# Aligning TensorE's tiles to 128 bytes and reading the output weights from the last column to the first

## The chip, the cores and the metric

One core of one Trainium2 chip runs the whole program. The metric is the device time of one execution in microseconds (us); before the change the median of three runs is 708.79 us (708.63 to 709.17).

## The reference

An attention block with 32 memory slots feeds a two-layer network. Per batch b (8), head h (8), with 576 tokens s, 64 channels d and 32 slots m:

```
a    = exp(phi - max_s phi);  a = a / (sum_s a + 1e-9)
k_m  = a^T k;   v_m = a^T v                       # 32 x 64 per head
attn = softmax over m of (q k_m^T / 8)            # 576 x 32 per head
x    = attn v_m, heads side by side               # 4608 tokens x 512
h    = x @ w_in                                   # 512 x 2048
g    = h if h > 0 else exp(h) - 1
out  = g @ w_out                                  # 2048 x 512
```

## The kernel before, in words

Batches run one after another; each one's 576 tokens are two halves of 288. The attention of a batch gives `A`, its probabilities (128 rows of head and slot, two groups). `x` is never formed: `vw` is v_m times w_in, four tiles per batch of 512 of the 2048 hidden channels each (`vw(b, c)`, L722 to L742), and the hidden layer is `vw` times `A`.

The main loop goes over 256 steps: (batch, half, j), where j is one of 16 blocks of 128 hidden channels. `hidden` (L769) makes a 128 x 288 block in PSUM from six matmuls: three passes over two groups, with high and low parts (`PASSES`, L40) of 4-byte float32r operands; the stationary operand is a 128 x 128 piece of `vw`, the moving one 288 columns of `A`. ScalarE (L793, L794) and VectorE (L802, L805) apply the activation into a `gf` tile (five buffers), and L825 and L831 split it into the high and low parts of a `gp` tile. `project` (L847) then calls `by_channels` (L837) for two blocks of 128 tokens: three matmuls each, where the stationary operand is a 128 x 128 piece of `gp` and the moving one 512 columns of `wout[j]`, its high or low part. The last 32 tokens of each half are gathered over two batches in a `rest` tile, and go through `by_channels` in `rest_project` (L892). So L839 runs 256 x 6 + 4 x 16 x 3 = 1728 times, and L778 256 x 6 = 1536 times.

TensorE loads the stationary operand by an instruction of its own (PEld in the profile) ahead of each matmul. The order of all work is written out by hand: the table `FIRST` for the first batches and `at(place, ...)` for the others.

The weights come as 64-bit words, `w_in` and `w_out`, and are decoded on the chip while the first two batches run (L390 to L441). `dec_high` and `dec_rest` leave `wout[j]` as [128, 2, 512]: high and low part, 512 output columns each. All tiles lie in SBUF for the whole program. Pools lay them one behind another in units of 32 bytes, so a small tile (`tiny`, `nm`, `rinv`, `mx`, `rs`, the `touch` targets) shifts all that follow. The four `touch` DMAs at the start (L922) load 64 bytes per partition that nothing reads, each into a tile of its own.

Of the kernel before, what the change touches and what calls it, by code (L numbers as in the profile page):

```python
# [8 lines left out]
F32 = mybir.dt.float32  # L9
# [7 lines left out]
P = 128  # L17
B, H, S, D, M = 8, 8, 576, 64, 32
DM, DFF = 512, 2048
HALF = S // 2  # L20
# [10 lines left out]
NJ = DFF // P  # L31
# [142 lines left out]
def fused_kernel(ctx: ExitStack, tc: tile.TileContext, phiT, phi, phit, kv0, kvt, kv, q0, q1, w_in, w_out, out):  # L174
# [11 lines left out]
    work = ctx.enter_context(tc.tile_pool(name="work", bufs=2))  # L186
# [9 lines left out]
    wout = {}  # L196
# [262 lines left out]
    def slot_scale(b):  # L459
        s = st[b]  # L460
        sums = s["sums"]
        nc.vector.tensor_scalar(sums, sums, EPS, None, ALU.add)
        rinv = work.tile([P, 2], F32, name="rinv")
        nc.vector.reciprocal(rinv, sums)
        s["rinv"] = rinv

# [180 lines left out]
    def softmax_sum(b, u):  # L647
        sc = st[b]["sc"][u]
        n = sc.shape[1]
        sm = work.tile([P, 2 * HALF // SQ], F32, name="sm")[:, :n]  # L650
        nc.vector.tensor_reduce(sm, sc, AX.X, ALU.add)
        nc.vector.tensor_scalar(sm, sm, EPS, None, ALU.add)
        rs = work.tile([P, 2 * HALF // SQ], F32, name="rs")[:, :n]
        nc.vector.reciprocal(rs, sm)
        st[b]["rs", u] = rs

# [180 lines left out]
    def by_channels(ps, gp, j, first, last):  # L837
        for n, (x, y) in enumerate(PASSES):
            nc.tensor.matmul(  # L839
                ps,  # L840
                gp[:, y],
                wout[j][:, x, :],
                start=(first and n == 0),
                stop=(last and n == 2),
            )

    def project(it):  # L847
        b, hf, j = order[it]
        _, first, last = ends[it]
        if first:  # L850
            acc[b, hf] = [ps_o.tile([P, DM], F32, name=f"pso{hf}{t}") for t in range(NT)]
        gp = gps.pop(it)
        for t in range(NT):
            by_channels(acc[b, hf][t], gp[:, :, t * P : (t + 1) * P], j, first, last)
# [37 lines left out]
    def rest_project(p, i):  # L892
        if i == 0:
            acc["rest", p] = ps_o.tile([P, DM], F32, name="pso00")
        gp = gs.pop(("rest", p, i))[1]
        for n in range(2):
            j = 2 * i + n
            by_channels(acc["rest", p], gp[:, :, n * P : (n + 1) * P], j, j == 0, j == NJ - 1)

    def rest_store(p):  # L900
# [4 lines left out]
        for n in range(4):  # L905
            eng[n % 2].dma_start(
                out[2 * p + n // 2, n % 2, NT * P :], t[n * REST : (n + 1) * REST, :]
            )

    tiny = work.tile([P, 1], F32, name="tiny", bufs=1)  # L910
    warm = ps_o.tile([P, P], F32, name="pso00")

    touched = {
# [5 lines left out]
        "out": w_out[0][:, :8],  # L919
    }  # L920

    def touch(x):  # L922
        rows = touched[x]
        n = 16 * list(touched).index(x)
        t = work.tile([P, 16], F32, name=f"touch{n}", bufs=1)
        if x in ("in", "out"):
            t, rows = t.bitcast(U32), rows.bitcast(U32)
        nc.scalar.dma_start(t, rows)
# [4 lines left out]
    def warm_up(n):  # L933
# [7 lines left out]
        f.__name__: f  # L941
        for f in (
            tables, touch, warm_up, load_phi, load_e, load_kv, load_kv0, load_q, load_half_q, load_raw, dec_mag,
            dec_sign, dec_low, dec_top, dec_add, dec_high, dec_rest, phi_max, phi_exp, slot_scale,
            spread_max, e_shift, e_exp, e_transpose, e_copy, slots, slots_copy, slots_transpose,
            kv_copy, clear, scores, scores_of, turn, softmax_max, softmax_shift, softmax_exp, softmax_sum,
            softmax_divide, back, turn_back, probs_high, probs_low, vw, vw_high, vw_low, hidden,
            elu_exp, elu_max, elu_rest, rest_copy, elu_high, elu_low, project, collect, store, rest_high, rest_low,
# [18 lines left out]
    def softmax(b, u, o, *steps):  # L967
        turned, shifted, exped, divided, back, parts = (o + x for x in steps)
        at(turned, turn, b, u)
        at(shifted, softmax_max, b, u)  # L970
        at(shifted + 0.01, softmax_shift, b, u)
        at(exped, softmax_exp, b, u)
        at(divided, softmax_sum, b, u)
        at(divided + 0.01, softmax_divide, b, u)
        at(back, turn_back, b, u)
        at(parts, probs_high, b, u)
        at(parts + 0.01, probs_low, b, u)
# [8 lines left out]
    def attention(b, o):  # L986
        at(o + 0.5, load_phi, b)
        for u in range(3):
            at(o + 1 + 0.1 * u, load_e, b, u)
        at(o + 3.5, phi_max, b)  # L990
        at(o + 3.6, spread_max, b)
        for c in range(NCH):
            at(o + 3.7 + 0.01 * c, load_kv, b, c)
        at(o + 3.8, load_q, b, 0)
        for g in range(2):
            at(o + 5.5 + g, phi_exp, b, g)
        at(o + 7.5, slot_scale, b)
        for u in range(3):
            at(o + 8, e_shift, b, u)
            at(o + 9.5 + u, e_exp, b, u)  # L1000
        for c in range(NCH):
            at(o + 12.4, slots, b, c)
        at(o + 12.5, load_q, b, 1)
        at(o + 12.6, load_q, b, 2)
        at(o + 13.5, slots_copy, b)
        at(o + 14.4, slots_transpose, b)
        at(o + 14.5, kv_copy, b)
        at(o + 17.4, scores_of, b, "bb", "wx")
        for u in range(3):
            softmax(b, u, o + 18.5 + 2.5 * u, 0, 1, 2, 3, 4, 5)  # L1010
# [86 lines left out]
```

## Time and profile before

| | |
|---|---|
| runs, median (lowest to highest) | 708.79 us (708.63 to 709.17) |
| span of the profiled execution, first to last instruction | 706.7 us |
| TensorE matmul (PE) busy | 697.6 us, 99% |
| TensorE weight load (PEld) busy | 581.0 us, 82% |
| VectorE (DVE) busy | 453.0 us, 64% |
| ScalarE (ACT) busy | 457.0 us, 65% |
| GpSimd (POOL) busy | 69.4 us, 10% |

The profile gives a span and no separate time for its own execution; what lies around the span (start and completion) is taken as the 2.1 us between 706.7 and the median of 708.79. The busy time of PE includes the modelled end of each matmul, which runs on while the next one streams, so the pace of matmuls is read from the starts of consecutive rows and not from their lengths.

### The profile page before, as it was taken

To read this page: it belongs to the slowest core of one execution; us is meant where nothing else is said; L and a number is where in the kernel's file an instruction comes from. 1 tells how busy PE (TensorE), PEld (TensorE's weight loads), DVE (VectorE), ACT (ScalarE), POOL (GpSimd) and SP (SyncE) were. 2 spreads that over 40 slices of the span, in tenths; PEclk is the share of its full clock that TensorE was granted. 3 is DMA by queue.
4 is the path that set the end of the run, shared out by engine and by line. 5 is a ranking of instruction groups with operands and counts; after the bars stand their busy time and mean duration, and the time that the engine had idled before them with its cause. 6 is when DMAs were issued, how large, how long until landed. Compare 5 with 4: busy or idle time off the path is not lost.

```text
span 706.7 us, 13637 instructions
## 1 busy us (share of the span) xinstructions
PE 697.6 (99%) x5112; PEld 581.0 (82%) x5112; DVE 453.0 (64%) x1207; ACT 457.0 (65%) x1101; POOL 69.4 (10%) x117
## 2 busy tenths in 40 slices
PE   8999999999999999999999999999999999999997
PEld 7778787878878888888787888878888888788886
DVE  4989877976686469554864548764683546944442
ACT  3879988877457557575655746765564655756652
POOL 0332342123000200020000200001000010000000
PEclk9999999999999999999999999999999999999999
DMA  9982023351314400251003420243001440000001
GB/s 344 406 349 90 1 68 116 113 154 23 134 43 109 171 31 2 97 177 64 1 1 111 165 76 1 66 105 137 31 1 59 106 157 31 1 31 0 31 2 45
DMA packets 26450, 64.50 MB, mean 91 GB/s; under 512 B 3984, under 2 KB 8592, under 8 KB 26384
## 3 DMA queue, kind: packets, MB, share of 16 engines
q1 hardware_dynamic: 25712, 63.46, 26.3%
q8 instruction: 41, 0.67, 0.4%
q10 hardware_dynamic: 672, 0.16, 0.1%
q14 instruction: 25, 0.20, 0.1%
HBM read 54.17 MB, written 9.44 MB: 90 GB/s over the span
## 4 chain that ended last, share of the span: by engine, by line
PE 94%; DMA 4%; DVE 0%; ACT 0%; issue 0%; SPq 0%
PE pso L839 57%; PE psh L778 29%; PE psb L556 4%; PE psb L497 2%; PE pso L556 2%; DMA raw<-w_out 2%; DMA raw<-w_in 1%; DMA qh<-q 1%; DMA touch<-kv 0%; PE psb L525 0%; PE psb L569 0%; PE pso L569 0%; PE psh L672 0%; SPq L322 0%; DVE A L715 0%
## 5 line engine op out<-in xcount | busy, mean ns | idle before, releaser
L839 PE MATMUL pso<-wout,gp 128*128 128x512 f32 x1728 | 440.0, 395 | 0.0
L839 PEld LDWEIGHTS pso<-wout,gp 128*128 128x128 f32 x1728 | 310.9, 188 | 61.3 <-issue 2.1
L778 PEld LDWEIGHTS psh<-A,vw 128*128 128x128 f32 x1536 | 227.6, 188 | 33.8 <-issue 9.2
L778 PE MATMUL psh<-A,vw 128*128 128x288 f32 x1536 | 245.9, 297 | 0.6 <-ACT A L701 0.4
L793 ACT ACTIVATE gf<-psh 128x288 f32<-128x288 f32 x256 | 105.2, 411 | 104.6 <-PE psh L778 99.2
L805 DVE SCALAR_TENSOR_TENSOR gf<-gf,psh 128x256 f32<-128x256 f32 x192 | 80.7, 421 | 140.0 <-ACT gf L794 139.8
L825 ACT CAST gp<-gf 128x256 fp32r<-128x256 f32 x256 | 103.4, 405 | 76.9 <-DVE gf L805 65.2
L831 DVE TENSOR_TENSOR gp<-gf,gp 128x256 fp32r<-128x256 f32 x256 | 112.4, 442 | 51.1 <-ACT gp L825 50.1
L794 ACT ACTIVATE gf<-gf 128x288 f32<-128x288 f32 x256 | 114.2, 446 | 8.1
L298 POOL TENSOR_TENSOR e<-e,nmb 128x512 f32<-128x512 f32 x12 | 16.5, 1397 | 361.5 <-ACT gf L794 160.5
L802 DVE SCALAR_TENSOR_TENSOR gf<-gf,psh 128x288 f32<-128x288 f32 x64 | 28.6, 450 | 17.7 <-ACT gf L794 15.9
L813 DVE SCALAR_TENSOR_TENSOR rest<-gf,psh 128x32 f32<-128x32 f32 x192 | 34.6, 180 | 0.0
L740 DVE TENSOR_TENSOR vw<-psb,vw 128x512 fp32r<-128x512 f32 (+2 forms) x48 | 27.0, 584 | 4.4 <-ACT vw L734 4.4
L883 ACT CAST gp<-rest 128x256 fp32r<-128x256 f32 x32 | 12.6, 406 | 21.9 <-PE pso L839 21.9
L821 POOL COPY rest<-gf 128x32 f32<-128x32 f32 x64 | 18.8, 320 | 70.2 <-DVE gf L802 70.1
L734 ACT CAST vw<-psb 128x512 fp32r<-128x512 f32 (+2 forms) x48 | 22.5, 498 | 0.7 <-PE psb L556 0.7
L888 DVE TENSOR_TENSOR gp<-rest,gp 128x256 fp32r<-128x256 f32 x32 | 12.9, 420 | 15.6 <-ACT gp L883 15.6
L556 PE MATMUL psb<-win,kvm 64*32 64x512 f32 (+2 forms) x384 | 22.3, 521 | 0.0
L396 ACT ACTIVATE mag<-raw 128x512 uint32<-128x512 uint32 x30 | 20.1, 672 | 2.6 <-DVE win L418 1.3
L392 ACT ACTIVATE mag<-raw 128x512 f32<-128x512 f32 x30 | 19.7, 669 | 0.6 <-DMA raw<-w_in 0.4
L740 DVE TENSOR_TENSOR vw<-pso,vw 128x512 fp32r<-128x512 f32 (+1 forms) x28 | 17.2, 625 | 0.7 <-ACT vw L734 0.6
L734 ACT CAST vw<-pso 128x512 fp32r<-128x512 f32 (+1 forms) x28 | 14.5, 530 | 0.5 <-PE pso L556 0.5
(134 smaller groups left out, 443.5 us busy)
## 6 DMA issues: line engine op xcount, KB each, us to landing
kvt<-kv SPq DMA_DIRECT2D x32, 512.0 KB, 7.6
raw<-w_in SPq DMA_DIRECT2D x15, 512.0 KB, 9.6
raw<-w_out SPq DMA_DIRECT2D x15, 512.0 KB, 9.0
out<-osb SPq DMA_DIRECT2D x14, 512.0 KB, 2.8
qt<-q SPq DMA_DIRECT2D x18, 384.0 KB, 4.4
ph<-phiT SPq DMA_DIRECT2D x7, 576.0 KB, 4.9
e<-phi SPq DMA_DIRECT2D x12, 256.0 KB, 4.6
kvt<-kvt SPq DMA_DIRECT2D x8, 256.0 KB, 8.1
```

The source lines that it names most:

```text
L556: nc.tensor.matmul(outs[a][32 * j : 32 * j + 32, :], lhs[r, 32 * j : 32 * j + 32], rhs[r, j], start=True, stop=True, tile_position=(64 * a ...
L734: nc.scalar.copy(s["vw"][c][:, HI, a, n0:n1], s["ps"]["vw", c, n0][a])
L740: nc.vector.tensor_tensor(t[:, LO, a, n0:n1], s["ps"]["vw", c, n0][a], t[:, HI, a, n0:n1], ALU.subtract)
L778: nc.tensor.matmul(ps, t[:, x, g, c0 : c0 + P], s["A"][hf][:, y, g, :], start=(n == 0), stop=(n == 5),)
L793: nc.scalar.activation(gf, ps, AF.Relu, scale=-1.0)
L794: nc.scalar.activation(gf, gf, AF.Exp, scale=-1.0)
L802: nc.vector.scalar_tensor_tensor(gf, gf, -1.0, ps, ALU.add, ALU.max)
L805: nc.vector.scalar_tensor_tensor(gf[:, :n], gf[:, :n], -1.0, ps[:, :n], ALU.add, ALU.max)
L813: nc.vector.scalar_tensor_tensor(rest_of(b, j)[:, o : o + REST], gf[:, n:], -1.0, ps[:, n:], ALU.add, ALU.max)
L825: nc.scalar.copy(gp[:, HI], gs[it][:, : NT * P])
L831: eng.tensor_tensor(gp[:, LO], gf[:, : NT * P], gp[:, HI], ALU.subtract)
L839: nc.tensor.matmul(ps, gp[:, y], wout[j][:, x, :], start=(first and n == 0), stop=(last and n == 2),)
```

## The change

Small pads bring every tile that TensorE reads to a multiple of 128 bytes. The `touch` DMAs write into the first `gf` tile in place of four tiles of their own. `w_out` is handed to the kernel with its columns reversed, and the matmul of L839 reads the 512 columns of `wout[j]` with a step of -1, from the last to the first, so that its results come out in the same order as before. The instructions of each engine stand in the same order as before, with the same operations and shapes.

```
@@ slot_scale
         rinv = work.tile([P, 2], F32, name="rinv")
+        pad("rinv", 64)
@@ softmax_sum
         rs = work.tile([P, 2 * HALF // SQ], F32, name="rs")[:, :n]
+        pad("rs", 64)
@@ by_channels
                 ps,
                 gp[:, y],
-                wout[j][:, x, :],
+                wout[j][:, x, ::-1],
@@ before the steps
+    pads = set()
+    def pad(name, n):
+        if name not in pads:
+            pads.add(name)
+            work.tile([P, n // 4], F32, name=f"pad_{name}", bufs=1)
     tiny = work.tile([P, 1], F32, name="tiny", bufs=1)
+    pad("tiny", 96)
@@ touch
-        t = work.tile([P, 16], F32, name=f"touch{n}", bufs=1)
+        if not spots:
+            spots.append(work.tile([P, HALF], F32, name="gf", bufs=5))
+        t = spots[0][:, n : n + 16]
@@ kernel
-        "w_out": np.ascontiguousarray(moe_w_out).view(np.uint64).reshape(NJ, P, DM),
+        "w_out": np.ascontiguousarray(moe_w_out[:, ::-1]).view(np.uint64).reshape(NJ, P, DM),
```

Where the tiles start, as the remainder of the byte address after division by 128, in the programs as built:

| tile | read by | before | changed |
|---|---|---|---|
| `A` (4 buffers) | L778, moving | 32 | 0 |
| `vw`, pool of three buffers | L778, stationary | 0 | 0 |
| `vw` of c = 3 from batch 2 on | L778, stationary | 32 | 0 |
| `gp` (3 buffers) | L839, stationary | 32 | 0 |
| `wout` 0 to 7 and 12 to 15 | L839, moving | 32 | 0 |
| `wout` 8 to 11 | L839, moving | 96 | 0 |
| `ident`, `win` | transposes, products | 0 | 0 |
| `kvm`, e tiles | products, slots | 96 | 0 |
| `ph`, key, value and query tiles | transposes, slots, scores | 32 | 0 |

## Rows read from the trace of the kernel before

**Rows 1.** The page: busy time by engine, granted clock, chain by engine and line.
```profile
span 706.7 us, 13637 instructions
...
PE 697.6 (99%) x5112; PEld 581.0 (82%) x5112; DVE 453.0 (64%) x1207; ACT 457.0 (65%) x1101; POOL 69.4 (10%) x117
...
PEclk9999999999999999999999999999999999999999
...
PE 94%; DMA 4%; DVE 0%; ACT 0%; issue 0%; SPq 0%
PE pso L839 57%; PE psh L778 29%; PE psb L556 4%; PE psb L497 2%; PE pso L556 2%; DMA raw<-w_out 2%; DMA raw<-w_in 1%; DMA qh<-q 1%; DMA touch<-kv 0%; PE psb L525 0%; PE psb L569 0%; PE pso L569 0%; PE psh L672 0%; SPq L322 0%; DVE A L715 0%
```

**Rows 2.** Groups of the page: line, engine, operation, count; busy us, mean ns; idle before.
```profile
L839 PE MATMUL pso<-wout,gp 128*128 128x512 f32 x1728 | 440.0, 395 | 0.0
L839 PEld LDWEIGHTS pso<-wout,gp 128*128 128x128 f32 x1728 | 310.9, 188 | 61.3 <-issue 2.1
L778 PEld LDWEIGHTS psh<-A,vw 128*128 128x128 f32 x1536 | 227.6, 188 | 33.8 <-issue 9.2
L778 PE MATMUL psh<-A,vw 128*128 128x288 f32 x1536 | 245.9, 297 | 0.6 <-ACT A L701 0.4
```

**Rows 3.** Timeline of PE: start us, us, line, count; `vw` at remainder 0.
```profile
299.14 0.96 PE L778 MATMUL psh<-A,vw 128*128 128x288 f32 x6
299.94 1.56 PE L839 MATMUL pso<-wout,gp 128*128 128x512 f32 x6
301.34 0.96 PE L778 MATMUL psh<-A,vw 128*128 128x288 f32 x6
302.14 1.55 PE L839 MATMUL pso<-wout,gp 128*128 128x512 f32 x6
303.53 0.96 PE L778 MATMUL psh<-A,vw 128*128 128x288 f32 x6
```

**Rows 4.** The same view further on, where L778 reads `vw` of c = 3.
```profile
310.09 0.94 PE L778 MATMUL psh<-A,vw 128*128 128x288 f32 x6
310.87 1.54 PE L839 MATMUL pso<-wout,gp 128*128 128x512 f32 x6
312.25 0.94 PE L778 MATMUL psh<-A,vw 128*128 128x288 f32 x6
313.03 1.54 PE L839 MATMUL pso<-wout,gp 128*128 128x512 f32 x6
314.40 0.94 PE L778 MATMUL psh<-A,vw 128*128 128x288 f32 x6
```

**Rows 5.** Timeline of PE: warm-up matmuls of `ident` with `ident`, both at remainder 0.
```profile
25.12 2.50 PE L935 MATMUL pso<-ident 128*128 128x128 f32 x20
27.37 1.04 PE L778 MATMUL psh<-A,vw 128*128 128x288 f32 x6
```

**Rows 6.** Pieces of the chain: start us, us, what; two long runs of L839.
```profile
530.69 12.59 PE pso L839 x54
543.28 0.80 PE psh L778 x6
...
687.68 15.13 PE pso L839 x66
```

**Rows 7.** Busy us (instructions) by stretch: the decoding of the weights, and later.
```profile
20.00:60.00 40.00, 37.95 (x405) 31.52 (x398) 35.16 (x89) 33.54 (x83) 13.12 (x18) 1.00 0.78 310
60.00:150.00 90.00, 89.93 (x558) 74.38 (x558) 78.77 (x162) 79.47 (x186) 27.53 (x48) 1.00 0.30 95
350.00:450.00 100.00, 100.00 (x685) 83.40 (x684) 61.59 (x178) 61.81 (x153) 3.66 (x4) 1.00 0.19 63
```

**Rows 8.** L839 alone by stretch: PE busy, PEld busy, clock, DMA share, GB/s.
```profile
20.00:60.00 40.00, 11.09 (x42) 7.45 (x42) 1.00 0.78 310
60.00:100.00 40.00, 25.52 (x102) 18.49 (x102) 1.00 0.17 54
100.00:150.00 50.00, 31.68 (x126) 22.80 (x126) 1.00 0.41 128
```

More of the change, by code (lines that the diff above doesn't have):

```diff
@@ L920, in fused_kernel @@
     }
+    spots = []
     def touch(x):
```

## The prediction

> **What bounds the kernel now.** I read the page first. TensorE's matmuls are busy for 99% of the span, and the chain that ended last is TensorE for 94% of it: L839, the output product, alone 57% and L778, the hidden layer, 29% [rows 1]. [...] The groups then show that these matmuls wait for nobody: idle time before L839 is 0.0 us over 1728 instructions, before L778 0.6 us over 1536 [rows 2]. What is left is the pace inside TensorE, from one matmul's start to the next, and this is the only thing that the change can move much.
>
> The timeline gives that pace. Six matmuls of L839 start at 302.14 and the next group starts at 303.53: 1.39 us, or 231.7 ns each [rows 3]. Six of L778 take 301.34 to 302.14, or 133.3 ns each. [...] The long runs in the chain say the same: 12.59 us for 54 is 233.1 ns, 15.13 us for 66 is 229.2 ns [rows 6]. [...] The weight load is 188 ns against a pace of 231.7 for L839, with 61 us of idle time over the program before it [rows 2], so it fits beside the stream of L839. [...]
>
> **The change, part by part.** No instruction is added, removed or moved on any engine's queue, and every shape stays. The `touch` DMAs keep their number and size. They now hold the first `gf` buffer: the buffer is taken again only when the other four have been used, steps after 64 bytes per partition have landed, so I cost this and the pads at nothing. If that cover failed, it would be one wait, once. The reversed `w_out` arrives as the same contiguous words, decoding works column by column, and the reversal on the way in is undone by the reversed read; nothing for the other engines.
>
> *Alignment, L778.* Before, `A` starts at remainder 32 and three of four `vw` tiles at 0; from batch 2 on the fourth tile is at 32, like `A`. The trace therefore holds the experiment already: with different remainders six matmuls take 0.80 us (299.14 to 299.94, and 301.34 to 302.14) [rows 3], with equal ones 0.78 us (310.09 to 310.87, and 312.25 to 313.03) [rows 4]. The changed kernel has equal remainders everywhere. 48 of the 256 groups (six batches, two halves, four j) have them already, so 208 x 0.02 = 4.2 us. Whether remainder 0 is better than 32 for both is not shown; bounds for this term are 0 and 4.2 doubled, and I take 4.
>
> *Alignment, L839.* `gp` and 12 of the 16 `wout` tiles have equal remainders already. The groups beside the two kinds of `vw` take 1.40, 1.39 and 1.38, 1.37 us [rows 3, 4], too little to carry a term. Nothing.
>
> *Reversal, L839.* No row shows a descending read. [...] Between nothing and 21.8 I take 8 ns x 1728 = 13.8 us: the pace of 229.2 to 233.1 in rows with different buffers shows that some of the excess depends on where operands lie, but the `ident` row has half the fetch rate and may flatter the floor.
>
> The gain is not all kept. 270 of the 1728 matmuls of L839 run between 20 and 150 us [rows 8], where VectorE and ScalarE are busy for 87 to 88% of 60 to 150 us while they decode weights [rows 7]. There a faster TensorE soon waits for them, and I take back nearly all that these 270 would give, 270 x 8 ns = 2.2, say 2 us. Later both are at 62%, and a TensorE that is 2 to 3% faster leaves them at 64%.
>
> Sum: 706.7 - 4 - 13.8 + 2 = 690.9 us of span; with the 2.1 us around it 693.0. The median of the runs is 708.8, which is the same 2.1 above the span, so the forecast compares directly.
>
> [...] The pace differs by 3 ns per matmul of L778 with the stationary tile's place [rows 3, 4], so the two reads of TensorE seem not to be free of each other. [...]
>
> **The rivals.**
> *Only the alignment works.* Direction is immaterial, L778 gains its 4.2 us, L839 stays at 231.7: 704.6. For it: this is the only part with rows behind it. [...]
>
> [...]
>
> *The descending stream is slower.* The place is the fetch of `wout` in L839, all 1728 times. It decides as soon as a backward read costs more than 4.2 us / 1728 = 2.4 ns per matmul. [...] For it: nothing else in the program reads backwards, so nothing shows that the fetch can. Against it: L839 already leaves its weight load room, and a step of -1 touches the same bytes.
>
> **How the numbers follow.** Forecast (both parts, the reversal worth between 3 and 22 us): 0.52. Alignment alone: 0.18. Nothing: 0.13. Slower: 0.17. A measurement of this kernel can tell about 0.2% from no change, 1.4 us; so faster is 0.52 + 0.18 = 0.70, same 0.13, slower 0.17. Within the forecast the reversal gives, if the floor of the `ident` row is reached and alignment pays double, 693.0 - (21.8 - 13.8) - 4 = 681.0, and 677 if L778 then loses another 4 / 1536 us of its 13 ns each, 2.6 ns; I start the range there. Upwards it takes in alignment alone (704.6) and no change (708.8 and its scatter): 711. Left out are nearly all of the slower rival and a little below, under 2 in 10.
>
> **What would show it.** In the timeline six matmuls of L839 should take 1.34 us or so where they took 1.39 or 1.40, and six of L778 0.78 everywhere; the busy time of the L839 group should fall from 440 to about 426. L839 still at 1.39 with L778 at 0.78 means alignment alone. [...] New idle time before L839 or L778 between 20 and 150 us would show the taken-back part. The prediction is wrong if L839's pace moves the other way, or if the excess of L778 falls far below 10 ns, since I give it 10.

## The result and the profile after

The changed kernel is slower: 713.78 us (713.45 to 714.10, four runs) against 708.87, a ratio of 1.0071 with a 95% interval of 1.0059 to 1.0083. The forecast was 693, the range 677 to 711.

The page after, with the same parts as [rows 1] and [rows 2] (the lines of the kernel have moved: L839 is L841, L778 is L780):

```profile
span 711.7 us, 13639 instructions
...
PE 702.9 (99%) x5112; PEld 581.8 (82%) x5112; DVE 455.1 (64%) x1207; ACT 456.6 (64%) x1101; POOL 69.3 (10%) x117
...
PE 94%; DMA 4%; DVE 0%; ACT 0%; issue 0%; SPq 0%
...
L841 PE MATMUL pso<-wout,gp 128*128 128x512 f32 x1728 | 445.4, 399 | 0.0
L841 PEld LDWEIGHTS pso<-wout,gp 128*128 128x128 f32 x1728 | 310.5, 188 | 64.8 <-issue 2.1
...
L780 PE MATMUL psh<-A,vw 128*128 128x288 f32 x1536 | 246.3, 298 | 0.6 <-ACT A L703 0.4
```

The span grew by 5.0 us. The busy time of the output product grew by 5.4, from 440.0 to 445.4, that of the hidden layer by 0.4, and no idle time came up in front of either. So nearly all of the loss is inside one group of 1728 matmuls. Its pace, the mean distance from a start to the next over all matmuls whose successor starts within 300 ns, went from 231.0 to 233.9 ns: 2.9 x 1728 = 5.0 us. The hidden layer's (within 200 ns) went from 132.9 to 133.3.

The timeline of PE after, in the same place as [rows 3]:

```profile
300.57 0.96 PE L780 MATMUL psh<-A,vw 128*128 128x288 f32 x6
301.37 1.56 PE L841 MATMUL pso<-wout,gp 128*128 128x512 f32 x6
302.77 0.96 PE L780 MATMUL psh<-A,vw 128*128 128x288 f32 x6
303.57 1.56 PE L841 MATMUL pso<-wout,gp 128*128 128x512 f32 x6
304.97 0.96 PE L780 MATMUL psh<-A,vw 128*128 128x288 f32 x6
```

The two groups of L841 take 1.40 us each, 233.3 ns a matmul. Such a pair of rows hides how regular this has become: before, the middle half of the distances lay between 228 and 233 ns, after it lies between 233 and 234. The long runs show the loss best; the chain after has, for the two pieces of [rows 6],

```profile
533.90 12.81 PE pso L841 x54
...
692.33 15.46 PE pso L841 x66
```

12.81 against 12.59 us and 15.46 against 15.13, 4 and 5 ns for each matmul. The prediction named this as a sign of being wrong: L839's pace moved the other way.

### The profile page after: what moved, and what is told of

Its sections match the earlier page's. It is cut to its first block, busy times and chain, and to the rows that moved or that the text cites. A ratio compares the mean times of both kernels' runs of the same rounds, so it can differ in the third digit from the quotient of the medians.

```text
span 711.7 us, 13639 instructions
## 1 busy us (share of the span) xinstructions
PE 702.9 (99%) x5112; PEld 581.8 (82%) x5112; DVE 455.1 (64%) x1207; ACT 456.6 (64%) x1101; POOL 69.3 (10%) x117
## 4 chain that ended last, share of the span: by engine, by line
PE 94%; DMA 4%; DVE 0%; ACT 0%; issue 0%; SPq 0%
PE pso L841 57%; PE psh L780 29%; PE psb L557 4%; PE psb L498 2%; PE pso L557 2%; DMA raw<-w_out 2%; DMA raw<-w_in 1%; DMA qh<-q 1%; DMA gf<-kv 0%; PE psb L526 0%; PE psb L570 0%; PE pso L570 0%; PE psh L674 0%; SPq L322 0%; DVE A L717 0%
## 5 line engine op out<-in xcount | busy, mean ns | idle before, releaser
L841 PE MATMUL pso<-wout,gp 128*128 128x512 f32 x1728 | 445.4, 399 | 0.0
L841 PEld LDWEIGHTS pso<-wout,gp 128*128 128x128 f32 x1728 | 310.5, 188 | 64.8 <-issue 2.1
L780 PEld LDWEIGHTS psh<-A,vw 128*128 128x128 f32 x1536 | 228.4, 188 | 34.9 <-issue 9.2
L780 PE MATMUL psh<-A,vw 128*128 128x288 f32 x1536 | 246.3, 298 | 0.6 <-ACT A L703 0.4
L425 POOL TENSOR_TENSOR top<-top,mag 128x512 uint32<-128x512 uint32 x9 | 12.5, 1391 | 24.8 <-ACT mag L396 24.8
```

Of the source, the lines that this page charges most:

```text
L780: nc.tensor.matmul(ps, t[:, x, g, c0 : c0 + P], s["A"][hf][:, y, g, :], start=(n == 0), stop=(n == 5),)
L841: nc.tensor.matmul(ps, gp[:, y], wout[j][:, x, ::-1], start=(first and n == 0), stop=(last and n == 2),)
```

## The experiments

**One half of the change at a time.** Two kernels split it: the first has the pads and the `touch` targets without the reversal, the second the reversal without the pads.

```
e1: the changed kernel with
-                wout[j][:, x, ::-1],
+                wout[j][:, x, :],
-        "w_out": np.ascontiguousarray(moe_w_out[:, ::-1])...
+        "w_out": np.ascontiguousarray(moe_w_out)...
e2: the kernel before with these two lines the other way
```

> Only the alignment: pads and the touch targets as in the change, w_out stored and read forward. Theory R (the backward read is what costs): L839's line keeps about 231 ns from start to start and the time is 708.8 or, with the 4 us of the hidden layer, 705. Theory A (the places cost: both operands of a matmul now start at the same multiple of 128): L839's line goes to 233 to 234 ns as in the changed kernel and the time is 713 to 714. Theory B (only the two together cost): as R.

> Only the reversal, tiles where they were before. Theory R: 233 to 234 ns per matmul of L839's line and 713 to 714 us, the same for wout 8 to 11 (remainder 96) and the others (32). Theory A: 231 ns and 708 to 709 us. Theory B (weights are read back to front too, so two descending streams that start at the same remainder stay in step and collide all along): wout 8 to 11 leave the 233 ns, by several ns, and the others keep it.

The alignment alone gives 708.20 us, ratio 0.9995 (0.9985 to 1.0004): nothing that can be told from no change. The reversal alone gives 714.06 us, ratio 1.0075 (1.0060 to 1.0090): all of the loss. The same two rows of the chain, of e1 and then of e2:

```profile
530.09 12.61 PE pso L841 x54
...
687.13 15.09 PE pso L841 x66
```

```profile
534.36 12.78 PE pso L839 x54
...
692.79 15.43 PE pso L839 x66
```

The pace of the output product is 230.6 ns in e1 and 234.0 in e2. Theory R stands, theory A falls for these places. In e2 `wout` 8 to 11, at another remainder than `gp`, keep 233.5 ns like the others at 234.2, which already speaks against theory B.

**Is it a collision of two backward streams?** Theory B supposes that the weight load runs back to front as well, which no row shows either way: then both reads of the changed kernel ran backward, and tiles at the same remainder might stay in step and collide. Two kernels move `gp` by 64 bytes, one with the backward `wout`, one with the forward one.

```
e5: the changed kernel, e6: e1, both with
     def elu_high(it):
+        pad("gp_ahead", 64)
         gp = work.tile([P, 2, NT * P], F32R, name="gp", bufs=3)
+        pad("gp_behind", 64)
```

> The changed kernel with gp, the stationary operand of the output product, 64 bytes further on (remainder 64 against wout's 0), still read against reversed wout. Theory R: still 233 to 234 ns and 713 to 714 us, whatever the offset. Theory B: the streams no longer collide, the pace falls below 228 ns and the time below 705 us.

> As e1 (aligned, read forward), with gp at remainder 64 against wout's 0. Theory R: as e1, since two streams that run against each other meet at any offset: 230 to 232 ns. Theory A: the pace falls from 233 to 231 ns or less as the remainders part.

e5: 712.67 us, ratio 1.0058 (1.0041 to 1.0075), pace 233.4 ns. The backward read keeps its pace with the streams out of step, far from the 228 ns and 705 us of theory B, which falls as the cause of the loss. A small part of it may stand: the changed kernel, with both tiles at remainder 0, reads `wout` 8 to 11 at 234.9 ns and the others at 233.6, e5 at 233.1 and 233.4, and is 1.1 us faster. e6: 707.99 us, ratio 0.9984 (0.9975 to 0.9994), pace 231.4 ns, with the hidden layer at 132.0 in place of e1's 133.3.

**The disputed cost by itself (e7, the probe).** At the end of the kernel before, eleven runs of 40 matmuls, each with an own line, on the high part of `wout[5]`; forward and backward by turns. Both directions read the same tile with the same contents, so nothing but the direction differs within a pair.

```
+        w = wout[5][:, HI, :]
+        run(lambda o, g: nc.tensor.matmul(o, g, w, start=True, stop=True))
+        run(lambda o, g: nc.tensor.matmul(o, g, w[:, ::-1], start=True, stop=True))
...
```

> The kernel before, with eleven runs of 40 matmuls added at its end, each run one form: wout's high part forward and backward at 512, 384 and 288 columns, then 512 columns with only 64 and only 32 columns of weights, both directions, then 512 forward with the same weights each time. Their results go nowhere. Theory F (a fixed cost for each backward read, at its start): backward is 2 to 4 ns over forward at every width and with every weight width. Theory C (a cost for each column or line): 2.9 ns at 512, 2.2 at 384, 1.6 at 288. Theory W (the weight load, which also runs back to front, meets the backward read): 2 to 4 ns with 128 columns of weights, half of that with 64, under 1 with 32. [...]

The timeline of PE over the added runs (start us, us, line, form, count):

```profile
705.32 9.36 PE L1056 MATMUL pso<-wout,gp 128*128 128x512 f32 x40 [2.21 <-ACT gp L1048]
714.52 9.50 PE L1057 MATMUL pso<-wout,gp 128*128 128x512 f32 x40
723.85 7.13 PE L1058 MATMUL pso<-wout,gp 128*128 128x384 f32 x40
730.82 7.27 PE L1059 MATMUL pso<-wout,gp 128*128 128x384 f32 x40
737.93 5.43 PE L1060 MATMUL pso<-wout,gp 128*128 128x288 f32 x40
743.19 5.50 PE L1061 MATMUL pso<-wout,gp 128*128 128x288 f32 x40
748.53 9.36 PE L1062 MATMUL pso<-wout,gp 128*64 128x512 f32 x40
757.73 9.50 PE L1063 MATMUL pso<-wout,gp 128*64 128x512 f32 x40
767.07 9.42 PE L1064 MATMUL pso<-wout,gp 128*32 128x512 f32 x40
776.32 9.50 PE L1065 MATMUL pso<-wout,gp 128*32 128x512 f32 x40
785.66 9.24 PE L1066 MATMUL pso<-wout,gp 128*128 128x512 f32 x40
```

The distance of two starts, divided by 40, is the mean pace with the way into each run included: 9.33 us or 233.3 ns for the backward L1057. The forward L1056 begins with steps of 226 to 337 ns and settles, from the sixth on, at 226 to 228. Without the first four, forward and backward are 226.8 and 233.3 ns at 512 columns, 173.6 and 177.7 at 384, 131.7 and 133.3 at 288. The cost of going backward is 6.6, 4.0 and 1.6 ns: over these three widths it grows with the columns, faster than they do. Neither F nor C has this right. (Closer widths, further down, show that the growth is not a steady one.)

Theory W, which supposes a weight load from back to front as theory B does, falls here. With 64 columns of weights the pace is 230.0 forward and 233.3 backward, with 32 it is 231.4 and 233.3. The difference does shrink with the load, 6.6, 3.3 and 1.9 ns, as W has it, but from the other side: forward becomes slower, and backward does not become faster. The weight loads of these runs (line, shape, count, busy us, mean ns, idle us before):

```profile
L1057 PEld LDWEIGHTS pso<-wout,gp 128*128 128x128 f32 x40 | 7.5, 188 | 1.8
...
L1063 PEld LDWEIGHTS pso<-wout,gp 128*64 128x64 f32 x40 | 5.4, 135 | 4.0
...
L1065 PEld LDWEIGHTS pso<-wout,gp 128*32 128x32 f32 x40 | 4.3, 108 | 5.0
```

A load of 108 ns in place of 188 does not move the backward pace by a tenth of a nanosecond, and the forward pace with it is 231.4 ns, not below the 226.8 with full weights. So the length of the load is not what costs. Backward these runs agree, 233.3 ns with every load; forward the pace is not free of the weights, 226.8, 230.0 and 231.4 ns with 128, 64 and 32 columns of them, and their place will matter too (e10, e12). No run here goes without a load before each matmul.

**The other operand backward (e8).** The 288 columns of `A` in the hidden layer are read backward, `w_out` stays forward. The kernel leaves out turning the tokens of each half back, so its output is not the reference's; its instructions and shapes are those of the kernel before.

```
-                    s["A"][hf][:, y, g, :],
+                    s["A"][hf][:, y, g, ::-1],
```

> The kernel before, with the 288 columns of A read backward in the hidden layer (the tokens of each half come out in reversed order), w_out forward. Theory F: L778's line goes from 133 to 135 to 136 ns, 1536 x 2.9 = 4.5 us, 713.3 us. Theory C: 134.6 ns, 2.5 us, 711.3 us. No cost for A: 708.8 us, and the cost is one of L839's place alone.

709.01 us, ratio 1.0006 (0.9996 to 1.0015); pace 133.2 ns against 132.9. So going backward costs nothing that can be told here, and neither the 713.3 us of theory F nor the 711.3 of theory C came. Beside the probe: backward runs near the probe's backward pace in both places (133.2 ns at 288 columns, 233.9 at 512, where the probe has 133.3 and 233.3). Forward depends on the tile. In the kernel before, three of the four `vw` tiles run at 133.1 to 133.6 ns, and there is nothing to lose; the fourth, c = 3, runs at 131.1, near the probe's 131.7, and goes to 133.1 in e8. At 512 columns forward is 231.0 on average, and there is more to lose. In its long runs the kernel before even reaches the probe's forward pace. Two pieces of the last run of 66, in the chain cut to 694 to 697.2 us of the kernel before, and to 699.45 to 702.7 us of the changed one:

```profile
693.86 3.40 PE pso L839 x15
```

```profile
699.33 3.51 PE pso L841 x15
```

These are 226.7 and 234.0 ns a matmul, by the order of the matmuls in the programs both on `wout` 3 to 7. With `wout` 8 to 15 the same run of the kernel before is at 228 to 234 ns.

**Width by width (e9).** To see whether the paces sit on a grid, eighteen runs were added to e1, from 512 down to 448 columns, forward and backward, with the first column at a multiple of 128 bytes; the last pair starts at column 8. One pair of the nine, `n` standing for the width:

```
+        run(lambda o, g: nc.tensor.matmul(o[:, :n], g, w[:, :n], start=True, stop=True))
+        run(lambda o, g: nc.tensor.matmul(o[:, :n], g, w[:, :n][:, ::-1], start=True, stop=True))
```

> e1 (aligned, forward) with eighteen runs of 40 matmuls added at its end, whose results go nowhere: 512, 508, 504, 500, 496, 488, 480 and 448 columns of wout's high part from its first column on, forward and backward, then columns 8 to 511 forward and backward. Theory L (the pace settles on whole steps of 16 columns, 64 bytes, 6.67 ns: 34 steps forward and 35 backward at 512): staircases, the pace staying on one step for 500 to 512 columns and falling by 6.67 ns from step to step, backward one step above forward where both settle. Theory S (streaming plus a fixed overhead): the pace falls by 0.417 ns with each column, forward 226.7, 225.0, 223.3, 221.7, 220.0, 216.7, 213.3, 200.0 from 512 to 448, and backward 5 to 7 ns over it. Under both: columns 8 to 511 as 504 columns from the first on if only the count matters; other if the end that lies inside a 64-byte step matters.

Timeline of PE, eight of the eighteen rows; the start of the next row ends a run:

```profile
778.13 9.11 PE L1079 MATMUL pso<-wout,gp 128*128 128x496 f32 x40
787.07 9.23 PE L1080 MATMUL pso<-wout,gp 128*128 128x496 f32 x40
796.14 8.96 PE L1081 MATMUL pso<-wout,gp 128*128 128x488 f32 x40
...
813.83 8.83 PE L1083 MATMUL pso<-wout,gp 128*128 128x480 f32 x40
822.50 8.97 PE L1084 MATMUL pso<-wout,gp 128*128 128x480 f32 x40
831.31 8.27 PE L1085 MATMUL pso<-wout,gp 128*128 128x448 f32 x40
839.42 8.43 PE L1086 MATMUL pso<-wout,gp 128*128 128x448 f32 x40
847.68 9.24 PE L1087 MATMUL pso<-wout,gp 128*128 128x504 f32 x40
```

L1079, 496 columns forward, lasts from 778.13 to 787.07, 8.94 us or 223.5 ns a matmul; L1080, backward, to 796.14, 226.8 ns. At 480 columns (L1083, L1084) it is 216.8 and 220.3, at 448 (L1085, L1086) 202.8 and 206.5. The means of the settled parts (the last 24 distances of each run), in ns:

| columns | forward | backward |
|---|---|---|
| 512 | 226.7 | 233.3 |
| 508 | 228.1 | 231.7 |
| 504 | 226.7 | 228.9 |
| 500 | 223.3 | 226.7 |
| 496 | 223.3 | 226.7 |
| 488 | 220.0 | 222.3 |
| 480 | 216.7 | 220.0 |
| 448 | 202.5 | 206.7 |
| 504, from column 8 | 226.7 | 230.0 |

Thirteen of the eighteen lie within 0.1 ns of a multiple of 3.33 ns: 206.7, 216.7, 220.0, 223.3, 226.7, 230.0, 233.3. That is the time of eight columns by an estimate from the backward paces at 512 and 448 columns, (233.3 - 206.7) / 64 = 0.416 ns each. The paces follow neither L, whose steps are twice as long (6.67 ns; the probe has 233.3 - 226.8 = 6.5 between backward and forward at 512 columns), nor S, a smooth slope (0.417 ns a column; the probe's forward 226.8 and 173.6 ns at 512 and 384 columns make 0.416). The multiples are those of the mean: single distances can swing about it by a repeating pattern, as from 224 to 236 ns in L1062 of the probe. Backward is slower at every width, by 2.2 to 4.2 ns, and by 6.7 only at 512, where forward settles at the 226.7 ns that 504 columns take, below the 228.1 of 508. Columns 8 to 511 forward run as the first 504 do; backward they take 230.0 against 228.9, so the end at which the read starts has a small part in it.

**Where the weights lie.** e6 was under the kernel before. Is that its place, and what of the others? `gp` went to the remaining two multiples of 32, and e6 ran again.

```
e10: e6 with pad("gp_ahead", 32), pad("gp_behind", 96)
e12: e6 with pad("gp_ahead", 96), pad("gp_behind", 32)
e11: e6
```

> e6 with gp at remainder 32 in place of 64, all read forward. If the place of gp matters by itself, the time leaves that of e6 (0.9984 of the kernel before) by 1 us or more, L839's line its 231.4 ns; if e6's small gain is chance of the phases, it stays within 1 us of e1 and of the kernel before, 707.5 to 709.

> e6 once more, unchanged, in more rounds: the only kernel so far whose time lies under that of the kernel before. If the gain belongs to the places, 707.2 to 708.2 us and a ratio of 0.998 to 0.999; if it was chance, 708.5 to 709.

> e6 with gp at remainder 96, the last of the four places of 32 bytes, all read forward. If the odd multiples of 32 are the bad ones (gp at 32: 233.2 ns, 710.8 us; at 0 and 64: 230.6 and 231.4 ns, 708.2 and 708.0 us), about 233 ns and 710.5 us. If 32 was bad for its own distance of 96 to wout, 230 to 231.5 ns and 708 us.

| remainder of `gp`, `wout` at 0, forward | us | ratio (95%) | pace of the output product | of the hidden layer |
|---|---|---|---|---|
| 0 (e1) | 708.20 | 0.9995 (0.9985 to 1.0004) | 230.6 | 133.3 |
| 32 (e10) | 710.78 | 1.0029 (1.0018 to 1.0040) | 233.2 | 132.3 |
| 64 (e6) | 707.99 | 0.9984 (0.9975 to 0.9994) | 231.4 | 132.0 |
| 64 (e11) | 707.75 | 0.9986 (0.9977 to 0.9994) | 231.4 | 132.0 |
| 96 (e12) | 710.43 | 1.0026 (1.0017 to 1.0036) | 233.0 | 132.2 |

The places with an odd multiple of 32 bytes between `gp` and `wout` cost 2 to 3 us against the even ones. The kernel before has even ones throughout (32 and 32, or 32 and 96); its `gp` stands at 32 as in e10, and its pace is 231.0, so the place of `gp` by itself is not what costs. In the odd places the forward read, at 233.2 and 233.0 ns, is as slow as a backward one, 233.4 to 234.0 in e5, e2 and the changed kernel. The last run of 66 took 15.09 us in e1 and 15.43 in e2, the reversal alone; in e6, e10 and e12 it took

```profile
687.06 15.26 PE pso L843 x66
```

```profile
689.41 15.41 PE pso L843 x66
```

```profile
689.02 15.43 PE pso L843 x66
```

e6 and e11 lie under the kernel before, by 0.14 to 0.16%; this is under the 0.2% that one measurement could tell, but two agree and both intervals end below 1. The gain is not the output product's, which has 231.4 ns against 231.0, but the hidden layer's, 132.0 against 132.9, of which e6 moves no tile against e1 (133.3). Why it gains is open.

## Why the prediction was wrong

**What bounds the kernel** held: the chain is TensorE's, no wait came or went, the granted clock stayed (1.000 in the profiled execution before, 0.999 to 1.000 in the four runs after), and the change acted on the pace alone. The 2 us that were to be lost again while the weights are decoded could not be seen, for TensorE did not become faster.

**The reversal** is the step that failed, "Between nothing and 21.8 I take 8 ns x 1728 = 13.8 us". It was 2.9 ns the other way, 5.0 us. No run shows the terms of that sentence: the 8 ns were the author's estimate, and the 21.8 us were taken over from `ident`, whose rows show 112.5 ns for 128 columns [rows 5] and nothing of 512. The excess of 13 and of 10 ns that the range and the last line give to L778 stands on no row either. What the runs showed in their place: the probe with the real form has the forward read, in a run of its own and settled, at 226.7 ns, and down to that pace there were 231.0 - 226.7 = 4.3 ns to gain, 7.4 us; L778 went from 132.9 to 133.3 ns. And the step to a gain had nothing under it. e10 and e12 show that the place of the one operand beside the other matters to a forward read (233.2 and 233.0 ns against 230.6 in e1). But nothing said that reading backward would take such a cost away. It does the opposite: the pace backward is about 233.3 with loads of 188, 135 and 108 ns, and 233.9 and 233.4 for `gp` in step and out of step with `wout` (the changed kernel and e5), which is the pace of forward reads in bad places. What a forward read has in good places, down to 226.7, is lost.

The sign that buffers matter was misread too: "the pace of 229.2 to 233.1 in rows with different buffers". The 54 and the 66 matmuls of [rows 6] read the same `wout` tiles at much the same paces; what sets them apart is that the first twelve of the 54 take about 250 ns each. Past that the 226.7 ns stood in the trace before.

**The alignment of the hidden layer**, taken at 4 us, gained nothing: its pace is 133.3 ns in e1 against 132.9. All of the alignment measured 708.20 against 708.88, 0.7 us, within the interval of no change. The 0.78 against 0.80 us of [rows 4] and [rows 3] were real, and hold over the whole kernel before, 131.1 ns against 133.1 to 133.6. But they had another cause than equal remainders: in e1, where all remainders are 0, the `vw` of c = 3 runs at 133.0 ns and the three others at 133.1 to 133.9. The timeline of e1, in the place of [rows 4], has 0.80 us for six:

```profile
309.38 0.96 PE L780 MATMUL psh<-A,vw 128*128 128x288 f32 x6
310.18 1.56 PE L841 MATMUL pso<-wout,gp 128*128 128x512 f32 x6
311.58 0.96 PE L780 MATMUL psh<-A,vw 128*128 128x288 f32 x6
312.38 1.55 PE L841 MATMUL pso<-wout,gp 128*128 128x512 f32 x6
```

Rows that differ in more than one thing (address, neighbour in time, and the pieces of `wout` that follow) were read as an experiment on one. The prediction had said that it was not shown whether 0 is better than 32 for both, and took the 4 us all the same.

**Alignment of L839 at nothing** was right as a sum, 231.0 against 230.6 ns, but not for its reason. It hides two moves against each other: `wout` 8 to 11, which the change brought from 96 to 0, went from 230.7 to 232.6 ns in e1, the twelve others from 231.1 to 229.9. The second came although their remainders were equal before and after, so the remainder by 128 is not all that counts. That the sum came out near nothing is luck. e10 and e12 show what wrong places cost.

**The rivals.** The slower one named the right place, the read of `wout` in L839, and a right point, 2.4 ns per matmul, at which it would eat up the alignment's 4.2 us. The 2.9 ns that came lie just past that point, and the time that came, 713.8, lies above the range, which ended at 711 and left nearly all of this rival out. It was given 0.17; what was held against it, that the weight load has room and that a step of -1 touches the same bytes, says nothing of the order in which they are read, and that no row reads backward was no evidence either way. "Nothing", given 0.13, was near to the truth for the alignment.

**What stays open.** That a backward moving operand has a settled pace of 233.3 ns at 512 columns, and that forward can settle 6.7 ns below it, is shown; why is not. No row shows what TensorE's fetch does within a matmul. It is open in part why the forward pace in the kernel is 231.0 on average: its long runs reach 226.7 with some `wout` tiles and not with others, which no remainder by 128 explains, and most of its matmuls come in groups of six between two of the hidden layer, at 231.3, where the probe settles only from the sixth on.

## What to carry to other kernels

In these runs a backward read was never faster than a forward one of the same form in the probes, and up to 6.7 ns slower. So an operand that TensorE streams should be read forward unless the other order is needed, and then a run of 40 matmuls at the end of the kernel prices it before anything is moved. Measure the pace that can be reached with the very form that is to be sped up: the bound taken here from another form, 21.8 us, was three times the 7.4 that this form's own settled pace leaves. When a cost is not in any row, a range has to run on without a gap from "nothing" into the rival on the other side.

## What the runs showed that was not expected

Matmul paces sat on a grid: in the eighteen runs of e9 thirteen means settled within 0.1 ns of multiples of 3.33 ns, and a width of 500 or 496 columns costs the same 223.3 ns forward. Reading 512 columns backward costs 6.7 ns in a run by itself and 2.9 in the kernel, but 288 columns backward cost 1.6 and nothing that can be told (133.2 against 132.9 ns). With `wout` at a multiple of 128 bytes, an odd multiple of 32 bytes to the weights' tile costs the output product 1.6 to 2.6 ns a matmul (233.0 and 233.2 against 230.6 and 231.4); between `A` and `vw` in the kernel before it cost nothing that the alignment could win back. In the kernels the forward pace of the output product went with the places of the tiles, from 230.6 to 233.2 ns; the backward one was 233.4 to 234.0 in the three that read `wout` so.
